# One load of 128 tokens on one queue, or two halves of 64 on two queues, at the start of a SwiGLU feed-forward kernel

## The chip, the cores and the metric

The kernel runs on one core of a Trainium2 chip. The metric is the time on the device in microseconds (us); the kernel before has three runs, and their median is 120.64 us. Beside them stands one profiled execution, whose trace gives the time of each instruction and of each load. Unless something else is said, a time with two decimals is counted from the start of that execution's span.

## The reference

For 2048 tokens x of width 512, gate and up weights of 512 x 1376 and down weights of 1376 x 512, all in bf16:

```
def reference(x, w_gate, w_up, w_down):
    g = _silu(x @ w_gate)
    u = x @ w_up
    return (g * u) @ w_down
```

## The kernel before, in words

TensorE needs the tokens with the model width on the partitions (xT_sb), since it contracts over partitions. The 1376 features are worked in tiles of 128 (ft 0 to 9, and a rest of 96), the tokens in four chunks c of 512. For each chunk and feature tile there is a group G (gate) and a group U (up), each of four accumulating matmuls over the four parts dk of the model width, into one of eight PSUM banks. ScalarE applies silu to the gate bank, VectorE multiplies it with the up bank and stores the hidden tile. After all chunks come the down matmuls, the copies of the outputs and their stores.

What concerns the change is the start, where no data is there yet:

- **Loads.** There are two queues from which the start's loads are issued. ScalarE's (loads_on_scalar, L119) has gate 0, that is the gate weights of feature tile 0, and then xn1. SyncE's (loads_on_sync, L123) has xn0, up 0, gate and up 1, gate and up of tiles 2 and 3 (here gate 2 and up 2), the transposing loads x0b and x0c (tokens 256-383 and 384-511), gate and up of tiles 4 to 6 (gate 4, up 4), of 7 to the end (gate 7, up 7), the last 32 up columns, the transposing loads of chunks 1 to 3, and the down weights. Each engine issues in this written order. ScalarE then loads its activation table and runs a dummy activation (L277) before its first copy.
- **Tokens 0-255.** xn0 (tokens 0-127) and xn1 (128-255) come as plain rows into xn_sb, 128 tokens on 128 partitions, 512 columns of bf16, and are transposed by TensorE: transposes(i) at L355 waits for xn{i} and does four matmuls with the identity into PSUM, which VectorE (dk 0 and 2) and ScalarE (dk 1 and 3) copy to xT_sb (L300 and L288).
- **TensorE's order** is written out by hand (L351 to L377). It first multiplies ones with ones: N_WARM = 5 of 512 columns, N_FILL = 2 of 128. Then come the lines below, where first[0] is G of tile 0, first[1] U of tile 0, and HT is 256 columns. A group's matmuls wait for their weights and for their tokens (need, L306, and after, L313).

```
            transposes(0)
            warm(N_GAP, P)
            gu_matmuls(first[0], 0, P)
            transposes(1)
            gu_matmuls(first[1], 0, P)
            gu_matmuls(first[0], P, HT)
            gu_matmuls(first[1], P, HT)
            for at in (2, 3, 4, 6, 5, 7):
                gu_matmuls(first[at], 0, HT)
```

After these come the columns 256-511 of the eight first groups: first[0] and first[1] for x0b, then both for x0c, then the other six for both; then all further groups with 512 columns at a time. The weight load (PEld) with which a matmul begins is the instruction that shows a wait in the trace. Each load raises a semaphore of its own by 16 when it has landed whole, and TensorE waits for 16 times the number of transfers.

Of the kernel before, what the change touches and what calls it, by code (L numbers as in the profile page):

```python
# [14 lines left out]
def bass_standalone__swiglu_ffn__prompt_kernel(nc, x, w_gate, w_up, w_down, out):  # L15
    _, S, D = x.shape
    F = w_gate.shape[1]
    P = 128
# [23 lines left out]
    xf = x[0]  # L42
# [8 lines left out]
    with ExitStack() as es:  # L51
# [19 lines left out]
        xn_sb = sb("xn_sb", [P, NXN, D], BF16)  # L71
# [10 lines left out]
        loads = {}  # L82

        def load_sem(name):
            loads[name] = sem(f"s_{name}")
            return loads[name]
# [6 lines left out]
        def load_x(eng, name, t0, t1):  # L93
            eng.dma_start_transpose(
                xT_sb[:, :, t0:t1], xf[t0:t1, :]
            ).then_inc(load_sem(name), 16)

        def load_w(eng, name, src, base, f0, f1):
            eng.dma_start(
                w_sb[:, :, base + f0:base + f1],  # L100
                src[:, f0:f1].rearrange("(k p) f -> p k f", p=P),
            ).then_inc(load_sem(name), 16)
# [4 lines left out]
        def load_gate(eng, a, b):  # L107
            load_w(eng, f"wg{a}", w_gate, 0, a * P, min(b * P, F))

        def load_up(eng, a, b):  # L110
            load_w(eng, f"wu{a}", w_up, UPH, a * P, min(b * P, F - 32))

        def load_xn(eng, i):
            eng.dma_start(xn_sb[:, i, :], xf[i * P:(i + 1) * P, :]).then_inc(load_sem(f"xn{i}"), 16)

        def out_rows(t):
            return of[t * P:(t + 1) * P, :]

        def loads_on_scalar(act):  # L119
            load_gate(act, *slabs[0])  # L120
            load_xn(act, 1)

        def loads_on_sync(sp):  # L123
            load_xn(sp, 0)
            load_up(sp, *slabs[0])
            for a, b in slabs[1:3]:
                load_gate(sp, a, b)
                load_up(sp, a, b)
            load_x(sp, "x0b", HT, HT + P)
            load_x(sp, "x0c", HT + P, SC)  # L130
            for a, b in slabs[3:]:
                load_gate(sp, a, b)
                load_up(sp, a, b)
            load_w(sp, "wut", w_up, F - (F - 32), F - 32, F)
            for c in range(1, NSC):
                load_x(sp, f"x{c}", c * SC, (c + 1) * SC)
            sp.dma_start(
                wd_sb[:, 0:NFF, :], w_down[0:NFF * P, :].rearrange("(k p) d -> p k d", p=P)
            ).then_inc(load_sem("wd"), 16)
            load_sem("wdt")  # L140
            for y0 in (0, 64):
                sp.dma_start(wd_sb[y0:y0 + 64, T01, :], w_down[NFF * P:F - SR, :]).then_inc(loads["wdt"], 16)
            for x0 in range(0, P, SR):
                sp.dma_start(wd_sb[x0:x0 + SR, T2, :], w_down[F - SR:F, :]).then_inc(loads["wdt"], 16)
            sp.dma_start(wd_sb[0:F_LAST, TAIL, :], w_down[NFF * P:F, :]).then_inc(load_sem("wdl"), 16)
# [19 lines left out]
        def tview(i, dk):  # L165
            return banks[KD * i + dk][:, 0:P // 2].bitcast(BF16)
# [47 lines left out]
        for i in range(NXN):  # L214
            for dk in range(KD):
                eng = "DA"[dk % 2]
# [16 lines left out]
        for at, t in enumerate(tiles):  # L233
            ob = at % NOS
            need = 16 * n_store[ob]
            parts = [(0, D)] if at < NST - 1 else [(0, LASTA), (LASTA, LASTB), (LASTB, D)]
            for c0, c1 in parts:
                g = add_group("O", t=t, c0=c0, c1=c1)
                eng = "A" if at % 2 == 1 and c0 == 0 else "D"
                op = add_op(  # L240
                    eng, g, kind="copy", out=o_sb[ob][:, c0:c1], src=g["bank"][:, 0:c1 - c0],
# [17 lines left out]
        def on_sync(sp):  # L259
            loads_on_sync(sp)  # L260
            store_tiles(sp, "S")
            for i in range(NOS):
                sp.wait_ge(s_out[i], 16 * n_store[i])
# [11 lines left out]
        def on_scalar(act):  # L275
            loads_on_scalar(act)
            act.activation(adummy[:, 0:4], zero_c, ACT.Silu)  # L277
            for op in act_ops:
                act.wait_ge(*ready(op))
                if op["kind"] == "silu":  # L280
                    if op["free"]:
                        act.wait_ge(s_D, op["free"])
                    fn = ACT.Silu
                else:
                    if op["stored"][1]:
                        act.wait_ge(*op["stored"])
                    fn = ACT.Copy
                act.activation(op["out"], op["src"], fn).then_inc(s_A, 1)  # L288
            store_tiles(act, "A")
# [13 lines left out]
        def on_tensor(pe):  # L303
            landed = set()

            def need(name, count=1):  # L306
                if name not in landed:
                    pe.wait_ge(loads[name], 16 * count)
                    landed.add(name)
# [43 lines left out]
            pe.wait_ge(s_I, 1)  # L353

            def transposes(i):  # L355
                need(f"xn{i}")
                for dk in range(KD):
                    pe.matmul(  # L358
                        tview(i, dk), lhsT=xn_sb[:, i, dk * P:(dk + 1) * P], rhs=ident[:, :],
                        start=True, stop=True, is_transpose=True,  # L360
                    ).then_inc(s_X, 1)

            first = groups[0:NB]
# [6 lines that stand above are left out]
# [142 lines left out]
```

## Time and profile before

| what | us |
|---|---|
| runs of the kernel before | 120.64, 120.75, 119.99; median 120.64 |
| profiled execution, its own time | 119.83 |
| its span, first to last instruction | 118.6 |
| TensorE busy in the span | 115.9 |
| first matmul on ones; first matmul of the first transposes | 0.84; 3.19 |
| second transposes' first weight load | 4.31 |
| mean granted TensorE clock | 1.00 |

The span is shorter than the execution's own time by what lies around the program's first and last instruction. The slices of the profile divide the span into 40 parts of 2.97 us, so the start up to tile 4 is in the first four of them. A busy share of TensorE of 98% says that there is hardly a hole in its row; it doesn't say that the matmuls go at their best rate. A load's time is given from the start of its issue to its landing, which is the last of the 16 increments of its semaphore, so a wait in the queue, the transfer and its confirmation are all in it.

### The profile page before, as it was taken

What the parts mean: (1) busy time and instruction counts of PE and PEld (TensorE: products, weight loads), DVE (VectorE), ACT (ScalarE), POOL (GpSimd) and SP (SyncE); (2) the same over time, 40 slices, a digit from 0 to 9 for tenths busy, and PEclk for the clock granted to TensorE, in tenths of its full rate; (3) what the DMA queues carried; (4) which work ended last, traced back from release to release, by engine and by line L of the source; (5) the groups of instructions that cost most, each with busy time, mean ns of one, the idle gap of its engine ahead of it and who ended that gap; (6) DMA issues with size and microseconds to landing.
All of it is one profiled execution on the core that took longest, in us unless ns stands there. A gap on an engine that the chain in (4) does not pass through costs nothing.

```text
span 118.6 us, 2344 instructions
## 1 busy us (share of the span) xinstructions
PE 115.9 (98%) x1019; PEld 59.9 (50%) x1019; DVE 38.0 (32%) x60; ACT 35.1 (30%) x62; POOL 1.1 (1%) x7
## 2 busy tenths in 40 slices
PE   7999999999999999999999999999999999999993
PEld 2888444444444444444444444444444445885442
DVE  0206443354433444424444244360000044003321
ACT  3407324353244272343263432330000033003021
POOL 1000000000000000000000000010000000000000
PEclk9999999999999999999999999999999999999999
DMA  3999999993000000000000000000000017200612
GB/s 90 288 199 325 270 145 236 243 357 76 0 6 0 0 0 0 0 3 3 0 0 6 0 0 0 0 0 6 0 6 0 0 58 237 69 0 6 209 56 88
DMA packets 17642, 8.83 MB, mean 75 GB/s; under 512 B 10624, under 2 KB 17632, under 8 KB 17632
## 3 DMA queue, kind: packets, MB, share of 16 engines
q1 hardware_dynamic: 16816, 8.33, 28.7%
q10 hardware_dynamic: 816, 0.36, 1.1%
q8 instruction: 8, 0.13, 0.5%
q14 instruction: 2, 0.02, 0.0%
HBM read 4.75 MB, written 2.10 MB: 58 GB/s over the span
## 4 chain that ended last, share of the span: by engine, by line
PE 98%; DVE 0%; issue 0%
PE bank L324 62%; PE bank L434 25%; PE bank L473 7%; PE bank L349 2%; PE bank L396 2%; PE bank L358 1%; DVE o_sb L300 0%
## 5 line engine op out<-in xcount | busy, mean ns | idle before, releaser
L324 PE MATMUL bank<-xT_sb,w_sb 128*128 128x512 bf16 (+2 forms) x384 | 73.4, 353 | 0.0
L324 PEld LDWEIGHTS bank<-xT_sb,w_sb 128*128 128x128 bf16 x384 | 36.2, 98 | 36.7 <-DMA w_sb<-in_w_gate_dram 0.2
L296 DVE TENSOR_TENSOR hT_sb<-sg_sb,bank 128x512 bf16<-128x512 f32 x40 | 27.5, 687 | 40.3 <-PE bank L324 39.3
L288 ACT ACTIVATE sg_sb<-bank 128x512 f32<-128x512 f32 x40 | 23.8, 596 | 40.6 <-PE bank L324 40.6
L434 PE MATMUL bank<-wd_sb,hT_sb 32*128 32x512 bf16 x496 | 29.0, 374 | 0.0
L434 PEld LDWEIGHTS bank<-wd_sb,hT_sb 32*128 32x128 bf16 x496 | 15.2, 93 | 11.6 <-issue 0.4
L300 DVE CAST o_sb<-bank 128x512 bf16<-128x512 f32 (+1 forms) x10 | 5.7, 594 | 31.1 <-PE bank L434 25.9
L288 ACT ACTIVATE o_sb<-bank 128x512 bf16<-128x512 f32 (+1 forms) x8 | 4.3, 582 | 33.6 <-PE bank L434 27.9
L473 PE MATMUL bank<-wd_sb,hT_sb 128*128 128x512 bf16 (+2 forms) x56 | 8.1, 304 | 0.0
L473 PEld LDWEIGHTS bank<-wd_sb,hT_sb 128*128 128x128 bf16 x56 | 4.2, 98 | 4.2 <-issue 0.4
L434 PE MATMUL bank<-wd_sb,hy_sb 32*128 32x512 bf16 (+1 forms) x32 | 5.0, 371 | 0.0
L296 DVE TENSOR_TENSOR hx_sb<-sgx_sb,bank 32x512 bf16<-32x512 f32 x4 | 2.8, 691 | 3.5 <-ACT sgx_sb L288 3.5
L349 PE MATMUL bank<-const-bfloat16-1.0 128*128 128x512 bf16 (+1 forms) x9 | 2.9, 486 | 0.8 <-PEq L497 0.8
L288 ACT ACTIVATE sgx_sb<-bank 32x512 f32<-32x512 f32 x4 | 2.4, 588 | 4.5 <-PE bank L324 4.5
L434 PE MATMUL bank<-wd_sb,hx_sb 32*128 32x512 bf16 (+1 forms) x16 | 3.0, 371 | 0.0
L288 ACT ACTIVATE sgy_sb<-bank 64x512 f32<-64x512 f32 x4 | 2.4, 590 | 0.1
L349 PEld LDWEIGHTS bank<-const-bfloat16-1.0 128*128 128x128 bf16 x9 | 1.1, 140 | 2.2 <-issue 2.2
L300 DVE COPY xT_sb<-bank 128x128 bf16<-128x128 bf16 x4 | 0.8, 221 | 4.1 <-PE bank L358 4.1
L396 PE MATMUL bank<-xT_sb,w_sb 128*64 128x512 bf16 x16 | 1.9, 382 | 0.0
L434 PEld LDWEIGHTS bank<-wd_sb,hy_sb 32*128 32x128 bf16 x32 | 1.6, 93 | 0.6
L277 ACT ACT_TABLE_LOAD x1 | 1.3, 1283 | 1.9 <-issue 1.9
L396 PEld LDWEIGHTS bank<-xT_sb,w_sb 128*64 128x64 bf16 x16 | 0.8, 109 | 1.0 <-DVE hT_sb L296 0.4
(15 smaller groups left out, 6.7 us busy)
## 6 DMA issues: line engine op xcount, KB each, us to landing
out_dram<-o_sb SPq DMA_DIRECT2D x15, 128.0 KB, 1.8
wd_sb<-in_w_down_dram SPq DMA_DIRECT2D x1, 1280.0 KB, 7.9
w_sb<-in_w_gate_dram SPq DMA_DIRECT2D x1, 480.0 KB, 5.8
w_sb<-in_w_up_dram SPq DMA_DIRECT2D x1, 448.0 KB, 6.5
w_sb<-in_w_gate_dram SPq DMA_DIRECT2D x1, 384.0 KB, 4.5
w_sb<-in_w_up_dram SPq DMA_DIRECT2D x1, 384.0 KB, 4.9
w_sb<-in_w_up_dram SPq DMA_DIRECT2D x2, 128.0 KB, 3.1
w_sb<-in_w_gate_dram SPq DMA_DIRECT2D x1, 256.0 KB, 3.5
```

Of the source, the lines that this page charges most:

```text
L277: act.activation(adummy[:, 0:4], zero_c, ACT.Silu)
L288: act.activation(op["out"], op["src"], fn).then_inc(s_A, 1)
L296: ins = dve.tensor_tensor(op["out"], op["a"], op["b"], ALU.mult)
L300: ins = dve.tensor_copy(op["out"], op["src"])
L324: return pe.matmul(bank[:, n0:n1], lhsT=w_sb[:, dk, col:col + P], rhs=xT_sb[:, dk, c * SC + n0:c * SC + n1], start=(dk == 0), stop=(dk == ...
L349: pe.matmul(banks[NB - 1][:, 0:width], lhsT=ones_w, rhs=ones_m[:, 0:width], start=True, stop=True)
L358: pe.matmul(tview(i, dk), lhsT=xn_sb[:, i, dk * P:(dk + 1) * P], rhs=ident[:, :], start=True, stop=True, is_transpose=True,).then_inc(s_X, 1)
L396: ins = pe.matmul(g["bank"][y0:y1, :], lhsT=w_sb[:, dk, YC0:YC0 + 64], rhs=xT_sb[:, dk, c * SC:(c + 1) * SC], start=(dk == 0), stop=(dk == ...
L434: ins = pe.matmul(g["bank"][:, 0:c1 - c0], lhsT=h, rhs=wd_sb[r0:r0 + SR, w, c0:c1], start=(start and fk == fks[0]), stop=(stop and fk == f ...
L473: ins = pe.matmul(g["bank"][:, 0:c1 - c0], lhsT=h, rhs=w, start=(last and fk == 0), stop=(fk == (NFF if last else NFF - 1)), skip_group_ch ...
```

## The change

xn1 is loaded by two transfers instead of one: rows 0-63 of the tile from SyncE's queue, directly behind xn0 and ahead of up 0, and rows 64-127 from ScalarE's queue, behind gate 0, where all of xn1 was. Both raise the same semaphore, and the second transposes wait until it has 32. All other instructions of the five engines are the same and in the same order; SyncE has one DMA issue more.

```
-        def load_xn(eng, i):
-            eng.dma_start(xn_sb[:, i, :], xf[i * P:(i + 1) * P, :]).then_inc(load_sem(f"xn{i}"), 16)
+        def load_xn(eng, i, p0=0, p1=P):
+            if p0 == 0:
+                load_sem(f"xn{i}")
+            eng.dma_start(xn_sb[p0:p1, i, :], xf[i * P + p0:i * P + p1, :]).then_inc(loads[f"xn{i}"], 16)
...
         def loads_on_scalar(act):
             load_gate(act, *slabs[0])
-            load_xn(act, 1)
+            load_xn(act, 1, P // 2, P)
 
         def loads_on_sync(sp):
             load_xn(sp, 0)
+            load_xn(sp, 1, 0, P // 2)
             load_up(sp, *slabs[0])
...
             def transposes(i):
-                need(f"xn{i}")
+                need(f"xn{i}", i + 1)
```

## The prediction

> **What bounds the kernel now.** I read the page's busy shares and slices first, then the chain that ended last, then the timeline of the first 14 us with the landing times of the loads, and last the stretches of those 14 us.
>
> ```profile
> PE 115.9 (98%) x1019; PEld 59.9 (50%) x1019; DVE 38.0 (32%) x60; ACT 35.1 (30%) x62; POOL 1.1 (1%) x7
> ...
> DMA  3999999993000000000000000000000017200612
> ...
> PE 98%; DVE 0%; issue 0%
> ```
>
> TensorE is the whole chain, and the DMA engines are full only in the first quarter. The change touches only loads of the start, so it can act only through waits of TensorE there. The timeline of the start (start, length, engine; PEld is the weight load with which each matmul begins, SPq and ACTq are DMA issues):
>
> ```profile
> 0.81 0.39 SPq L114 DMA_DIRECT2D xn_sb<-in_x_dram  x1
> ...
> 0.82 0.46 ACTq L99 DMA_DIRECT2D w_sb<-in_w_gate_dram  x1
> ...
> 1.26 0.42 SPq L99 DMA_DIRECT2D w_sb<-in_w_up_dram  x1
> 1.31 0.53 ACTq L114 DMA_DIRECT2D xn_sb<-in_x_dram  x1
> ...
> 2.82 0.51 SPq L99 DMA_DIRECT2D w_sb<-in_w_gate_dram  x1
> ...
> 3.92 2.60 SPq L94 DMA_TRANSPOSE xT_sb<-in_x_dram  x2
> ...
> 4.31 0.23 PEld L358 LDWEIGHTS bank<-ident,xn_sb 128*128 128x128 bf16 x4
> 4.50 1.69 PEld L324 LDWEIGHTS bank<-xT_sb,w_sb 128*128 128x128 bf16 x20
> ...
> 6.41 7.53 PEld L324 LDWEIGHTS bank<-xT_sb,w_sb 128*128 128x128 bf16 x68 [0.23 <-DMA w_sb<-in_w_gate_dram]
> 6.57 0.58 SPq L99 DMA_DIRECT2D w_sb<-in_w_gate_dram  x1
> ```
>
> The times from issue to landing of four of those loads, in order: xn1, up 0, gate 2 (feature tiles 2 and 3) and x0c (tokens 384-511):
>
> ```profile
> xn_sb<-in_x_dram ACTq DMA_DIRECT2D x1, 128.0 KB, 3.0
> ```
>
> ```profile
> w_sb<-in_w_up_dram SPq DMA_DIRECT2D x1, 128.0 KB, 3.2
> ```
>
> ```profile
> w_sb<-in_w_gate_dram SPq DMA_DIRECT2D x1, 256.0 KB, 3.5
> ```
>
> ```profile
> xT_sb<-in_x_dram SPq DMA_TRANSPOSE x1, 3.1
> ```
>
> Added to the issue starts they land at 4.3, 4.4, 6.3 and 8.4. The trace's own landing records give 4.27, 4.44, 6.37 and 8.39, which I use below; after one, the waiting weight load starts 0.04 later (6.37 to 6.41). Last the stretches; the figure ahead of GB/s is the DMA engines' share (overlapping packets take it over 1):
>
> ```profile
> 3.20:4.30 1.10, 1.10 (x12) 0.86 (x10) 0.44 (x2) 0.66 (x3) 0.00 (x0) 1.00 1.17 303
> ...
> 5.40:6.40 1.00, 1.00 (x12) 0.72 (x9) 0.00 (x0) 0.00 (x0) 0.00 (x0) 1.00 1.14 336
> 6.40:7.40 1.00, 1.00 (x10) 0.90 (x10) 0.00 (x0) 0.00 (x0) 0.00 (x0) 1.00 1.23 252
> 7.40:8.40 1.00, 1.00 (x14) 0.91 (x12) 0.00 (x0) 0.00 (x0) 0.00 (x0) 1.00 0.60 74
> ```
>
> From 3.2 to 7.4 the engines have no free time, so loads land by their place in the line of bytes, not by when they were issued. From 7.4 to 8.4 they run dry (0.60, 74 GB/s): there the loads wait for SyncE to issue. These two regimes decide the case.
>
> **The change part by part.**
>
> *xn1 lands earlier: gain at most 0.11.* The transposes of tokens 128-255 start at 4.31, right on xn1's landing at 4.27; the weight load before them is at 4.14. Successive 128-column matmuls go 0.107 apart while TensorE is slow (3.36, 3.47) and 0.056 apart later (4.38, 4.44), so without the wait they would start at 4.20 to 4.25: the wait is 0.06 to 0.11. After the change the first half stands on SyncE's queue right behind xn0 (landed 3.06) and lands before the second. The second still stands behind gate 0, as all of xn1 did, but is half as long: by the trace's packet records xn1's 1 KB packets ran from 3.1 to 3.85 among up 0's, half of them about 0.37, so it lands some 0.3 earlier, at about 3.95. The wait goes; I take the larger value, 0.11.
>
> *What is late next.* Up 0's first matmul (4.50) comes right on its landing at 4.44. Up 0 now stands behind 64 KB of x on its own queue and 64 KB on the other, before behind none and beside 128 KB: the bytes served up to its last one are the same, so it lands at 4.44 still, and its matmuls start at 4.49. The copies of the second transposes (at 4.58 to 5.09) come 0.11 earlier, so gate 0's second part, which waits for them at 4.86 and 5.14, ends some 0.1 earlier. Gate 1 (landed 4.85, used at 5.43) and up 1 (5.37, used at 5.87) do not bind, so TensorE reaches gate 2 at 6.20 instead of 6.30 (the weight load before is at 6.09, and 256 columns take 0.109 each twice over from there). But gate 2 lands at 6.37 whatever comes before: the same bytes stand ahead of it on full engines, and its issue at 2.82 has room (gate 1, issued at 1.73, had its first packets only at about 3.85, up 1 after it). So the matmuls start at 6.41 again. The gain is 0.11 at 4.3, and 0.00 at 6.41.
>
> *One more issue on SyncE.* It goes ahead of up 0, so all SyncE loads behind it slip by one slot: up 0, gate 1, up 1, gate 2, up 2, x0b, x0c, gate 4, up 4 and the rest. The nearest rows: xn0's slot of 0.45 (0.81 to 1.26) on the same queue for 128 rows, and the two 64-row loads later on the same queue:
>
> ```profile
> L142 SPq DMA_DIRECT2D wd_sb<-in_w_down_dram x2: 730/868/1007, 21.2 to 22.0; - x2
> ```
>
> So the slip is 0.45 to 1.05 (1.007 and a gap of 0.04). The first is of the same source, place and row length, with SyncE's queue still short; I take 0.45. Up 2 lands at 7.15 for use at 7.30 and x0b at 7.92 for use at 8.17, both with their issue well ahead on full engines: nothing. x0c lands at 8.39, and its first matmul is at 8.62 (weight load likewise): a spare of 8.62 - 0.04 - 8.39 = 0.19. Its issue ends at 6.53 and its packets end as the engines run dry. If they were held by the engines, a slip costs nothing; if by the issue, the cost is slip less spare, 0.26 at 0.45 and 0.86 at 1.05. It stands on the border of the two stretches, with most of its packets in the full one (1.23), so I let half the slip through, 0.23, for a cost of 0.04. Gate 4 (issued 6.57, engines dry) slips the whole 0.45: landed 11.08, used at 11.69, spare 0.57. Up 4: landed 12.12, used at 12.55, spare 0.39; with slip 0.45 it would be 0.06 late, but TensorE is by then late by the 0.04 of x0c; I count 0.02. Gate 7 and all behind have over a microsecond.
>
> *Shorter issue on ScalarE.* Behind xn1's issue (1.31, 0.53) come a table load (1.87 to 3.15), a dummy to 3.37, and the first copy at 3.60. That copy follows the transposes of xn0; spare 0.23. A half is at best shorter, at worst 1.01 by the row above: the copy 0.25 late, of which 0.11 is lost in the wait at 6.41, so 0 to 0.14. I take 0.
>
> *Gate 0 beside the first half of xn1.* 64 KB of packets now pass beside gate 0 (landed 3.49, first used at 3.83 after a copy that ended at 3.72): 128 KB take 0.43 at the 303 GB/s of the row, half takes 0.22, spare about 0.24. Taken as 0.
>
> *Do halves move as fast?* Same bytes, same 1 KB packets: 0. At worst a half takes as long as a whole, so both together 0.43 more on full engines, and gate 2 lands by that much later: 0 to 0.43. The trace has no 64-row load by itself in that stretch; the packets are xn1's own, so I take 0. [...]
>
> **Sum.** 0.00 + 0.04 + 0.02 = +0.06. The profiled execution took 119.83 (span 118.6 and 1.2 around it), so 119.89 by its clock; it lies 0.81 under the median of the three runs, 120.64 (119.99 to 120.75). Against the median: 120.7.
>
> **The rivals.**
>
> *A late x0c.* If x0c is held by its issue, and the slip is over 0.19, TensorE waits at 8.62. For it: the engines are dry from 7.5, and x0c's issue is the last thing before. Against it: share 1.23 in the stretch before. It gives 120.64 + 0.26 to 0.86 = 120.9 to 121.5; over 1% only together with the next.
>
> *Slow halves.* +0.43 at gate 2: 121.1. For it only the lack of a row; against it the same packets.
>
> *The slow clock of TensorE lasts longer* (the one on the other side, beyond what a measurement misses). The spacing halves from 0.107 to 0.056 at about 3.9, after 3 us of matmuls without a gap, though the granted clock reads 1.00 throughout. If gate 0's landing passes 3.73 and leaves a hole just there, and the faster spacing comes only after 6.4, then the 16 matmuls of 128 columns and 8 of 256 from 4.3 to 6.2 cost 16 x 0.051 + 8 x 0.107 = 1.7, less 0.3 of waits that they fill: +1.4, 122.0. For it: the spare is only 0.24. Against it: nothing ahead of 3.8 waits for the moved loads. [...]
>
> *The gain is kept.* If gate 2 comes earlier too, up to the whole 0.11 and what it waits there: 120.4. For it: runs in which TensorE comes to 6.4 later than here; against it: full engines.
>
> *The halves change nothing*, if the second lands at 4.27 as before: the sum is the same.
>
> **How the numbers follow.** Forecast (with the last case) 0.46; late x0c 0.15; slow halves 0.11; longer slow clock 0.08; gain kept 0.11; 0.09 for what no row names, 0.06 of it faster and 0.03 slower by over 1%. 1% is 1.2 us, about what a measurement of this kernel can tell from no change. Faster than 119.4: 0.06. Slower than 121.8: 0.08 + 0.03, and 0.03 for late x0c and slow halves at their upper ends together (1.3): 0.14. Within: 0.80. Range 119.9 to 121.4: below, the fastest of the shown runs; above, the upper end of the late x0c less 0.1; the runs' own spread of 0.76 is in it.
>
> **What would show it.** Right: the second transposes at 4.20 to 4.25, gate 2's matmuls at 6.41 with a longer wait, x0c's near 8.62 to 8.7, gate 4 landing 0.45 later, and the rest moved as one. Wrong: transposes still at 4.31 (no earlier landing), gate 2 landing much past 6.4 (slow halves), a weight-load wait on x0c near 8.6, or spacing of 0.107 past 4.4.

## The result, and the profile after

| | before | after |
|---|---|---|
| median of 9 runs each, us | 120.47 | 121.03 |
| lowest and highest, us | 119.99, 120.75 | 120.65, 121.29 |
| profiled execution, us | 119.83 | 120.91 |

The ratio is 1.0060 with a 95% interval of 1.0042 to 1.0077: slower by 0.4 to 0.8%. (The quotient of the two medians is 1.0046, inside that interval; nor are the ratios below, in general, quotients of medians.) Ratios leave out executions more than 1.5% above the fastest of the same kernel, which here are two of the run with both halves on ScalarE and no others. The chain of work that ended last, on the page of the changed kernel, is no longer TensorE alone. Here it is in order of time for the first 13 us (start, length, what):

```profile
0.81 0.40 SPq L116
...
1.27 0.54 SPq L116
...
1.86 0.57 SPq L99
...
2.48 0.51 SPq L99
...
3.03 0.51 SPq L99
...
3.58 3.83 DMA w_sb<-in_w_gate_dram
...
7.45 5.68 PE bank L327 x57
```

Before, this chain was TensorE from 0.84 on. Now it runs through SyncE's issues one after the other (xn0, the half of xn1, up 0, gate 1, up 1), then through the landing of gate 2, and only at 7.45 does it reach TensorE. The new issue, 0.54 and a gap of 0.05, stands in that chain. The timeline shows the same from TensorE's side:

```profile
1.86 0.57 SPq L99 DMA_DIRECT2D w_sb<-in_w_up_dram  x1
...
3.58 0.52 SPq L99 DMA_DIRECT2D w_sb<-in_w_gate_dram  x1
...
4.87 0.23 PEld L361 LDWEIGHTS bank<-ident,xn_sb 128*128 128x128 bf16 x4 [0.56 <-DMA xn_sb<-in_x_dram]
...
5.29 1.45 PEld L327 LDWEIGHTS bank<-xT_sb,w_sb 128*128 128x128 bf16 x20 [0.19 <-DMA w_sb<-in_w_up_dram]
...
7.45 6.48 PEld L327 LDWEIGHTS bank<-xT_sb,w_sb 128*128 128x128 bf16 x63 [0.71 <-DMA w_sb<-in_w_gate_dram]
```

Three waits, in brackets with what ended them: for xn1 (0.56), up 0 (0.19) and gate 2 (0.71). These instructions started at 4.31, 4.50 and 6.41 before. In this execution the last wait decides: what xn1 and up 0 cost would only have been waiting for gate 2. They are not free, though. Without the wait for gate 2 TensorE would have come to it at about 6.86 (an estimate: the last matmul ahead of it starts at 6.75, and such matmuls go 0.109 apart), 0.44 later than it did before. The stretches, with the DMA share ahead of GB/s, say why the loads are late:

```profile
3.20:4.30 1.10, 1.10 (x12) 0.90 (x10) 0.44 (x2) 0.69 (x3) 0.00 (x0) 1.00 0.71 165
...
5.40:6.40 1.00, 1.00 (x16) 0.96 (x16) 0.10 (x1) 0.24 (x2) 0.00 (x0) 1.00 0.91 244
6.40:7.40 1.00, 0.62 (x6) 0.31 (x4) 0.00 (x0) 0.00 (x0) 0.00 (x0) 1.00 1.14 321
7.40:8.40 1.00, 0.95 (x9) 0.75 (x10) 0.00 (x0) 0.00 (x0) 0.00 (x0) 1.00 1.29 201
```

From 3.2 to 4.3 the engines had 0.71 and 165 GB/s, where they had 1.17 and 303 GB/s before. They ran short of work, and the bytes that were not moved there came later.

One number ties a profile to its time. In the two profiles and in those of the twelve runs below, the execution's own time less the start of the first matmul on gate 2 is 113.40 to 113.52 us:

| kernel | gate 2 issued | landed | first matmul on it | execution | difference |
|---|---|---|---|---|---|
| before | 2.82 | 6.37 | 6.42 | 119.83 | 113.41 |
| after | 3.58 | 7.41 | 7.45 | 120.91 | 113.46 |
| before, once more | 2.82 | 6.72 | 7.16 | 120.57 | 113.41 |

So whatever a kernel here does to the time, it does before that matmul, and the 113 us behind it are the same to 0.12.

By this difference a median execution comes to gate 2 at about 7.06 before and 7.57 after (an estimate: the medians 120.47 and 121.03 less 113.41 and 113.46). The first profile of the kernel before, at 6.42, is one of its fastest executions, so the two profiles overstate the loss: 1.08 between them, 0.56 between the medians. In the median execution before, TensorE most likely reached gate 2 later than gate 2 landed (6.37 and 6.72 in the two profiles), as it did in the second one.

### The profile page after: what moved, and what is told of

It is laid out like the page before. It is cut to its first block, busy times and chain, and to the rows that moved or that the text cites. A ratio compares the mean times of both kernels' runs of the same rounds, so it can differ in the third digit from the quotient of the medians.

```text
span 119.6 us, 2345 instructions
## 1 busy us (share of the span) xinstructions
PE 116.2 (97%) x1019; PEld 59.8 (50%) x1019; DVE 38.0 (32%) x60; ACT 35.2 (29%) x62; POOL 1.1 (1%) x7
## 4 chain that ended last, share of the span: by engine, by line
PE 92%; DMA 3%; SPq 2%; issue 0%; DVE 0%
PE bank L327 59%; PE bank L437 25%; PE bank L476 7%; DMA w_sb<-in_w_gate_dram 3%; PE bank L399 2%; SPq L99 1%; SPq L116 1%; DVE o_sb L303 0%
```

## The experiments

All ratios are to the kernel before, run on the same chip; its medians there were 120.17 (first four), 120.26 (next four) and 120.38 (last four). The expected times of the first four reckon from 120.47, so 0.3 is to be taken off them.

**The slot alone.** Edit, against the kernel before:

```
             load_xn(sp, 0)
+            sp.dma_start(scr_sb[:, :], xf[0:64, 0:16]).then_inc(load_sem("scr"), 16)
             load_up(sp, *slabs[0])
```

> xn1 comes whole on ScalarE's queue as before; a transfer of 64 rows of 32 bytes into an unused tile (2 KB in all, extra work) goes on SyncE's queue ahead of up 0. Slot theory (the extra issue makes up 0 and all behind it late, and the DMA engines run dry meanwhile): the DMA share from 3.2 to 4.3 falls under 0.95 from 1.17, gate 2 lands at 7.0 to 7.4, TensorE waits there, and the time is 120.8 to 121.1 against 120.47. Halves theory (64-partition transfers of x move slowly and hold the engines): no bytes of x are in halves, so gate 2 lands at 6.4 to 6.5 and the time is 120.4 to 120.6.

Measured: 121.24, ratio 1.0082 (1.0055 to 1.0108). Three lines of its timeline, and the stretch:

```profile
1.26 0.54 SPq L126 DMA_DIRECT2D scr_sb<-in_x_dram  x1
...
3.57 0.51 SPq L100 DMA_DIRECT2D w_sb<-in_w_gate_dram  x1
...
7.33 6.69 PEld L327 LDWEIGHTS bank<-xT_sb,w_sb 128*128 128x128 bf16 x64 [0.46 <-DMA w_sb<-in_w_gate_dram]
```

```profile
3.20:4.30 1.10, 1.10 (x12) 0.91 (x10) 0.44 (x2) 0.66 (x3) 0.00 (x0) 1.00 0.82 203
```

2 KB ahead of up 0 take as long to issue as 64 KB do (0.54) and cost no less than the change does, as far as the intervals tell. No half of xn1 is needed for the loss. The loss is above what was expected, and the run doesn't say why.

**Both halves on ScalarE.** Edit, against the change:

```
             load_gate(act, *slabs[0])
+            load_xn(act, 1, 0, P // 2)
             load_xn(act, 1, P // 2, P)
...
             load_xn(sp, 0)
-            load_xn(sp, 1, 0, P // 2)
```

> Both halves of xn1 go on ScalarE's queue behind gate 0, SyncE's queue is as before. Slot theory: share from 3.2 to 4.3 near 1.1 and gate 2 at 6.4 to 6.5; only xn1's second half is issued a slot later on ScalarE (about 1.9) and lands at 4.4 to 4.8, of which some is lost in the wait for gate 2; time 120.4 to 120.8. Halves theory: the share falls under 0.95 as in the changed kernel, gate 2 lands past 7.0, time 121.0.

Measured: 121.18, ratio 1.0068 (1.0044 to 1.0091). Five of its eight executions took 120.87 to 121.28 and three 122.19 to 123.07; the profiled one is that of 122.19. Its chain:

```profile
1.31 0.54 ACTq L116
...
1.89 3.49 DMA xn_sb<-in_x_dram
...
5.43 0.61 PE bank L361 x4
```

The loss of this execution is another one: the second half, issued at 1.89 on ScalarE, lands at 5.38, TensorE's weight loads stand still for 0.91, and its matmuls of 256 columns still go 0.21 apart up to 8.6 (see the last section). Gate 2 lands at 6.77 and TensorE comes to it only at 8.78. Neither theory foresaw this; here it is xn1 that comes late, and the slow spacing makes more of it. What the five shorter executions lose was not profiled.

**xn1 whole on SyncE.** Edit, against the kernel before:

```
             load_gate(act, *slabs[0])
-            load_xn(act, 1)
...
             load_xn(sp, 0)
+            load_xn(sp, 1)
```

> xn1 goes whole on SyncE's queue ahead of up 0; ScalarE's queue has gate 0 alone. Slot theory: the same slot as in the changed kernel, so gate 2 lands past 7.0 and the time is 120.9 to 121.2, whatever xn1 itself does. Halves theory: no halves, share from 3.2 to 4.3 near 1.1, gate 2 at 6.4 to 6.6, time 120.3 to 120.6.

Measured: 120.62, ratio 1.0037 (1.0024 to 1.0050).

```profile
1.73 0.43 SPq L99 DMA_DIRECT2D w_sb<-in_w_up_dram  x1
...
7.04 0.77 PEld L324 LDWEIGHTS bank<-xT_sb,w_sb 128*128 128x128 bf16 x8 [0.43 <-DMA w_sb<-in_w_gate_dram]
```

Up 0 goes at 1.73 instead of 1.26: a whole tile takes 0.47 of SyncE, a half took 0.59. xn1 lands at 3.82, 0.45 earlier than before, and nothing comes of it. As many transfers as before, none in halves, and still a loss, at the low end of what was expected; that it is small because the slot is shorter is likely, not shown.

**The half behind up 0.** Edit, against the change:

```
             load_xn(sp, 0)
-            load_xn(sp, 1, 0, P // 2)
             load_up(sp, *slabs[0])
+            load_xn(sp, 1, 0, P // 2)
```

> As the changed kernel, but SyncE's half of xn1 goes behind up 0, ahead of gate 1. Slot theory: up 0 has its old place and fills the engines, only gate 1 and what is behind slip by the slot; the share from 3.2 to 4.3 is near 1, gate 2 lands at 6.4 to 7.0 and the time is 120.4 to 120.9. Halves theory: both halves still move slowly, share under 0.95, gate 2 past 7.0, 121.0.

Measured: 120.73, ratio 1.0037 (1.0021 to 1.0053). The share from 3.2 to 4.3 is 1.07; the hole comes one stretch later:

```profile
4.30:5.40 1.10, 0.66 (x10) 0.48 (x9) 0.30 (x2) 0.25 (x2) 0.00 (x0) 1.00 0.92 193
```

Gate 2 is issued at 3.49, lands at 7.11, a little later than expected, and is waited for. Up 0 in its old place fills the first hole, but the slip of the rest stays.

**A wait and no transfer.** Edit, against the kernel before (s_W is a new semaphore, and warm gets a third argument: the semaphore that its last matmul raises); the other two waits of this kind put s_W on the first or third matmul on ones:

```
-            warm(N_WARM, SC)
+            warm(2, SC, s_W)
+            warm(N_WARM - 2, SC)
...
             load_xn(sp, 0)
+            sp.wait_ge(s_W, 1)
             load_up(sp, *slabs[0])
```

> All transfers as in the kernel before; SyncE only waits, between xn0 and up 0, for the second matmul on ones (end about 1.9), so up 0 is issued at about 1.9 and all behind it 0.6 later, without a further transfer. Slip theory (a load lands some 3.6 to 3.8 after its issue starts, so the slip itself is the cost): gate 2 is issued at about 3.5 and lands at 7.0 to 7.4, time 120.6 to 121.1 against 120.17. Transfer theory (a further transfer costs by itself, by its completions or descriptors): no further transfer, gate 2 at 6.4 to 6.6, time 120.1 to 120.4.

Measured: 120.97, ratio 1.0053 (1.0036 to 1.0071).

```profile
1.88 0.40 SPq L100 DMA_DIRECT2D w_sb<-in_w_up_dram  x1
...
7.68 6.26 PEld L326 LDWEIGHTS bank<-xT_sb,w_sb 128*128 128x128 bf16 x62 [0.40 <-DMA w_sb<-in_w_gate_dram]
```

```profile
3.20:4.30 1.10, 1.10 (x13) 0.94 (x12) 0.44 (x2) 0.66 (x3) 0.00 (x0) 1.00 0.62 139
```

With the transfers of the kernel before, only 0.62 later, the hole (0.62, 139 GB/s), the late gate 2 (landed 7.64) and a loss like the change's are all there. This is the cleanest of the runs: the slip is enough.

**Up 0 and xn1 exchanged.** Edit, against the kernel before:

```
             load_gate(act, *slabs[0])
-            load_xn(act, 1)
+            load_up(act, *slabs[0])
...
             load_xn(sp, 0)
-            load_up(sp, *slabs[0])
+            load_xn(sp, 1)
```

> xn1 goes whole on SyncE's queue behind xn0, and up 0 in its stead on ScalarE's behind gate 0: as many transfers on each queue as before, none in halves. Slip theory: gate 1 and gate 2 keep their issue times (1.73, 2.82), gate 2 lands at 6.3 to 6.6, time 120.0 to 120.4. Transfer theory: the same, since there is no further transfer. Order theory (xn1's bytes ahead of up 0 on SyncE are the cost, as in the run with xn1 whole on SyncE): up 0 late, gate 2 past 6.9, time 120.6 or more.

Measured: 120.25, ratio 1.0002 (0.9986 to 1.0017). xn1's bytes ahead of the weights on SyncE cost nothing here, where no issue is added: gate 2 goes at 2.75 and lands at 6.44. TensorE waits 0.62 for up 0 at 5.18, but its matmuls go 0.056 apart from there, and it comes to gate 2 at 6.74, between the 6.42 and 7.16 of the two profiles of the kernel before.

**Halves by columns.** Edit, against the change (and the two calls likewise):

```
-            eng.dma_start(xn_sb[p0:p1, i, :], xf[i * P + p0:i * P + p1, :]).then_inc(loads[f"xn{i}"], 16)
+            eng.dma_start(xn_sb[:, i, d0:d1], xf[i * P:(i + 1) * P, d0:d1]).then_inc(loads[f"xn{i}"], 16)
```

> As the changed kernel, but xn1 is halved by columns: all 128 tokens, columns 0-255 on SyncE's queue ahead of up 0 and 256-511 on ScalarE's behind gate 0, each over 128 partitions. Slip theory: the slot ahead of up 0 is 0.45 to 0.6, gate 2 lands at 7.0 to 7.4, time 120.6 to 121.0. Halves theory (64 partitions move slowly): xn1 lands by 4.3 and gate 2 by 6.6, time 120.2 to 120.5.

Measured: 120.87, ratio 1.0050 (1.0035 to 1.0064).

```profile
5.31 8.62 PEld L327 LDWEIGHTS bank<-xT_sb,w_sb 128*128 128x128 bf16 x84 [0.65 <-DMA w_sb<-in_w_up_dram]
```

xn1 lands at 3.93 and gate 2 at 7.12. With all 128 partitions the halves do land early, the second transposes start at 4.29 without a wait, and the loss is there all the same. So the loss isn't that of 64 partitions; whether these add 0.1% to it, the intervals don't tell. In this execution the slip is met at up 0: it lands at 5.27, TensorE waits 0.65 for it, its matmuls go 0.107 apart until about 6.2, and it comes to gate 2 at 7.27, when that has landed.

**The change, with up 1 from GpSimd.** Edit, against the change:

```
             for a, b in slabs[1:3]:
                 load_gate(sp, a, b)
-                load_up(sp, a, b)
+                if a != 1:
+                    load_up(sp, a, b)
...
             ).then_inc(s_I, 1)
+            load_up(pool, *slabs[1])
```

> The changed kernel, with up 1 issued from GpSimd's queue instead of SyncE's, so that SyncE has as many issues ahead of gate 2 as before. Slip theory: gate 2 is issued at about 3.0 instead of 3.58 and lands at 6.6 to 6.9; what stays is xn1's own lateness; time 120.3 to 120.7 against 121.03 of the changed kernel. Transfer theory: as many transfers as in the changed kernel, gate 2 past 7.2 and time 120.9 or more.

Measured: 122.71, ratio 1.0205 (1.0187 to 1.0223). It does not test what it was made for: with up 1 on GpSimd's queue the other loads came later too.

```profile
1.86 4.61 DMA w_sb<-in_w_up_dram
...
6.52 6.50 PE bank L329 x60
```

Up 0, issued at 1.86 as in the change, now takes 4.61 to land, where it took 3.39; its own first packets come at 4.32. The trace's packet records show 4096-byte packets of GpSimd's queue from 3.84 on, of 0.16 to 1.03 us each, the first nine of 0.39 or more. Whether the slot given back would undo the loss was not settled by this run.

**A shorter and a longer wait.**

> As the run with a wait and no transfer, but SyncE waits for the first matmul on ones (end 1.43), so up 0 and all behind it are issued 0.2 later. Slip without spare (gate 2 already binds in the kernel before, so every slip is paid): gate 2 lands at 6.5 to 6.7, time 120.3 to 120.5 against 120.2. Full engines (a slip is free until the line of bytes runs out): gate 2 at 6.4, time 120.1 to 120.25.

> The same with a wait for the third matmul on ones (end 2.28), slip 1.05. Slip theory: gate 2 lands at 7.5 to 8.1, time 121.1 to 121.6, about 1 us over the kernel before; more if the wait of TensorE for up 0 comes near 1 us and its slow spacing of 0.107 lasts on, as in the runs with xn1's halves both on ScalarE. Transfer theory: 120.2 to 120.4.

Measured: 120.47, ratio 1.0016 (1.0000 to 1.0032), for a slip of 0.20; and 121.19, ratio 1.0068 (1.0047 to 1.0089), for 1.05. Gate 2 landed at 6.56 and 7.62. With the 0.62 of the middle wait the losses are 0.2, 0.6 and 0.8 us (ratio less one, times the median before): they grow with the slip. By the intervals they are 0 to 0.4, 0.4 to 0.9 and 0.6 to 1.1, so whether the longest slip is paid in full stays open; gate 2 came 3.77 after its issue there and 4.22 in the middle one. With the shortest wait TensorE came to gate 2 at 6.75, after it had landed, so that profile shows no wait for it.

**A slot behind x0c.** The transfer of the first experiment, moved:

```
             load_x(sp, "x0c", HT + P, SC)
+            sp.dma_start(scr_sb[:, :], xf[0:64, 0:16]).then_inc(load_sem("scr"), 16)
```

> The transfer of 2 KB of the run with the slot alone, but behind x0c and ahead of gate 4 on SyncE's queue. Slip theory with the spares of the trace: gate 4 and up 4 are issued 0.5 later, land at 11.5 and 12.6 for use at 11.7 and 12.55, so nothing to 0.1 is paid: 120.1 to 120.4 against 120.2. Transfer theory: a further transfer costs wherever it stands, 120.8 or more.

Measured: 120.29, ratio 0.9990 (0.9977 to 1.0003). The same 2 KB and a slot of much the same length (0.64) cost 0.8% ahead of up 0 and nothing behind x0c, where gate 4 and up 4 have spare. So it is not the number of transfers.

**The kernel before once more.**

> The kernel before once more, for a second profile: whether gate 2's landing near 6.4 and full DMA engines from 3.2 to 4.3 are this kernel's rule or one execution's luck. Slip theory: gate 2 at 6.3 to 6.7, share near 1.1, time 119.9 to 120.7. If the share is under 0.9 and gate 2 past 6.9 without any slip, the theory falls.

Measured: 120.57, one execution; gate 2 issued at 2.82, landed at 6.72. The share from 3.2 to 4.3 is 1.16, as in the first profile:

```profile
3.20:4.30 1.10, 1.10 (x12) 0.85 (x10) 0.44 (x2) 0.67 (x3) 0.00 (x0) 1.00 1.16 303
```

So full engines there are in both profiles of this kernel. But TensorE did not wait for gate 2; it came to it at 7.16, having been slow itself.

No version beat the kernel before by more than its interval. Gate 2 landed at 6.37 to 6.82 in the five profiles that issue it in its old place, and at 7.00 to 7.64 in the seven that issue it 0.47 or more later (the run with GpSimd left out). All these seven lost time; the exchange and the late slot, with gate 2 in its old place, lost none. Both halves on ScalarE lost too, in the profiled execution by xn1.

## Why the prediction was right in its range and wrong in its reason

The time, 121.03, lies in the range given, and the difference is under 1%, as the likeliest class said. The mechanism of the forecast failed, and with it its +0.06: what was measured is +0.56 between the medians. That the range held was luck: its upper end stood for a wait on x0c, which did not come, and it took in a loss from another place.

- *The step that failed:* "But gate 2 lands at 6.37 whatever comes before: the same bytes stand ahead of it on full engines, and its issue at 2.82 has room". It landed at 7.41. By the same reasoning up 0 was to land "at 4.44 still"; it landed at 5.25. The room was read from gate 1, "issued at 1.73, had its first packets only at about 3.85", as if gate 1 had been waiting in line. But xn0, with nothing ahead of it on its queue, has no packets for a while either: its first come 1.04 after the start of its issue (1.03 in the changed kernel). Up 0's come 1.1 to 1.7 after it in the twelve profiles that have it on SyncE and no load on GpSimd, also with the long wait, where the last packet before it on its queue ended at 2.87 and its own first came at 3.43. So a good part of the delay looks like a lead that each of these loads pays. Before, up 0's packets began at 2.81, when xn0's had just ended; in the changed kernel they begin at 3.31, and the engines run short (0.71 from 3.2 to 4.3). Nor did gate 2 land faster for being issued late: from issue to landing it took 3.55 to 3.99 in the five profiles that issue it in its old place, and 3.55 to 4.22 in the eight that issue it later. The shares before, 1.08 to 1.17 from 3.2 to 6.4, show that the engines were fed in time; they don't show by how much.
- *The slot.* Put at 0.45, measured at 0.59 (1.27 to 1.86). Gate 2 slipped by 0.75 at its issue: the slot, and a longer issue of up 0 (0.57 instead of 0.42).
- *xn1.* Forecast at about 3.95; it landed at 4.83, 0.56 after it was before, and the second transposes went from 4.31 to 4.87. The gain of 0.11 didn't come. That an early xn1 would have gained nothing is borne out: with column halves the transposes start at 4.29, and xn1 whole on SyncE has them at 4.24, both with a loss. But it was up 0 that TensorE waited for next (0.65 and 0.56), ahead of gate 2.
- *x0c.* It was given most of the price of the slip (0.04 of 0.06), and none was paid there: it landed at 9.28 for use at 9.69, since TensorE was later still. The wait came earlier in the same queue, at gate 2.
- *Gate 4 and up 4* cost nothing, after the change or with the late slot (0.9990), so up 4's 0.02 was not paid either. They were issued 0.87 and 0.88 later than before, and landed only 0.09 and 0.11 later, not the 0.45 that was given for gate 4: here, unlike at gate 2, a late issue was made up.
- *ScalarE's issue* was no shorter (0.55, before 0.53), and gate 0 landed 0.09 later (3.58), inside the spare of 0.24: both cost nothing, as said.
- *Slow halves.* This rival's 121.1 was near the time, and gate 2 past 6.4 was its sign. Its 0.43 was the author's estimate, 128 KB at 303 GB/s for a half that takes as long as a whole; no run shows that. The halves by columns, over all partitions, lose 0.50%, and the wait without a transfer 0.53%: the runs decide against it. Late landing of 64-partition halves did occur, in the changed kernel (xn1 at 4.83 instead of 4.27) behind the later gate 2; the runs leave its cause open.
- *A longer slow clock* did not decide in the changed kernel: after 4.9 the spacing is 0.056. It did occur in other runs (last section).
- *The halves change nothing* and *the gain is kept:* neither; the time of issue on SyncE's queue mattered (0.62 later and nothing else: 1.0053), not the bytes (2 KB ahead of up 0: 1.0082).

Open is how much of the 0.60% is due to the longer slot of a half (0.59 against 0.47 for a whole tile or a half by columns: 1.0060 against 1.0037 and 1.0050, intervals that overlap), and why gate 2 came between 3.55 and 4.22 after its issue in the thirteen profiles without GpSimd's load.

## What to carry to other kernels

Where a stream of loads feeds the start, count each issue on the queue that carries it as a term of the sum, for all that stand behind it, however few bytes it moves: here 2 KB took 0.54 to issue and cost 0.8%. Engines at a share of 1.17 did not make issue time free here: look for the lead between an issue and its first packets (1.04 for xn0, 1.1 to 1.7 for up 0), and move the slot in thought until a load comes too late. And find the one instruction behind which all profiles of a kernel are alike (here the first matmul on gate 2): then the search ends there. Two profiles are two executions; check their difference against that of the medians before giving a cause all of it.

## What the runs showed of the hardware that was not expected

**A transfer of 64 partitions took longer to issue on SyncE than one of 128.** For loads of x behind xn0: 0.54 for 64 rows (the change, the half behind up 0, and the 2 KB), 0.42 for 128 rows, whole or half as wide. The next issue was longer as well (up 0: 0.57 instead of 0.43). On the tile's own view of the change and of the run with column halves (shortest, median, longest in ns; the shortest is xn0's):

```profile
L116 SPq DMA_DIRECT2D xn_sb<-in_x_dram x2: 403/472/540, 0.8 to 1.3; - x2
```

```profile
L116 SPq DMA_DIRECT2D xn_sb<-in_x_dram x2: 401/408/416, 0.8 to 1.3; - x2
```

Second halves of 64 rows landed at 4.78 to 5.52 in four profiles; xn1 whole, or in column halves, at 3.82 to 4.43 where no 64-row transfer was in flight. With the 2 KB of 64 rows on SyncE, xn1 whole landed at 4.71 as well, so the reason need not lie in how fast a half's own bytes move; the runs leave it open.

**TensorE's slow spacing ended at different times in two executions of the same kernel, though the granted clock reads 1.00 in both.** Matmuls of 128 columns from 4.9 to 6.1 in the first profile of the kernel before, and in the second (count, busy time and mean ns of one):

```profile
L324 PE MATMUL bank<-xT_sb,w_sb 128*128 128x128 bf16 x9 | 0.9, 222 | 0.0
```

```profile
L324 PE MATMUL bank<-xT_sb,w_sb 128*128 128x128 bf16 x12 | 1.5, 314 | 0.0
```

The same kernel, 222 and 314 ns: in the first profile matmuls of 128 columns go 0.056 apart already from 4.32 to 4.72, in the second the slow spacing of 0.107 lasts to about 6.4, gate 2 is reached at 7.16 instead of 6.42, and the execution takes 0.74 longer, just that difference. This is much of the spread from 119.9 to 120.8 between runs of the kernel before, as far as two profiles can say. What sets the time of the step, the runs don't show. After waits of 0.91 (both halves on ScalarE) and 1.15 (up 1 from GpSimd) the slow spacing lasted to 8.6 and 9.05, in one profile each.
